# Fused attention and gated MLP on one core: one transfer out and four back for the reciprocals, new transfer durations in the planner, and a new order

## The chip, the cores and the metric

The kernel runs on one core of one Trainium2 chip. The metric is device time in microseconds, the median of several executions; lower is better. One execution was profiled, and its trace is read below.

## The reference, cut to what matters

There are 8 batches, 8 heads, 576 positions and a head size of 64; the MLP has d_model 512 and d_ff 1024. All arithmetic is in float32.

```python
q_rot, k_rot = (rotate(q), rotate(k))
scores = scale * np.matmul(q_rot, k_rot.transpose(0, 1, 3, 2))
scores = scores - np.max(scores, axis=-1, keepdims=True)
attn = np.exp(scores)
attn = attn / (np.sum(attn, axis=-1, keepdims=True) + 1e-09)
x = np.matmul(attn, v)            # then heads side by side: [8, 576, 512]
h = np.maximum(x @ w_in, 0.0)
u, v = (h[..., :d_ff // 2], h[..., d_ff // 2:])
v_n = (v - mu) / np.sqrt(var + 1e-06)
v_s = np.einsum('ts,bsd->btd', w_spatial, v_n) + b_spatial[None, :, None]
out = (u * v_s) @ w_out
```

## The kernel before

**The work.** The 64 heads are taken as 32 pairs, four pairs to a batch. A pair `i` loads its q and k (`st`, 576 KB each) and its values (`vr`), rotates them on GpSimd, splits them into a rounded high part and a rest, and copies the parts into the stacked operands `stk` by ten transfers inside SBUF. Its scores are nine tiles of 128 queries by 576 keys on TensorE (L782, for the first four pairs L802). VectorE takes the maximum of each row (L825), ScalarE the exponential and its row sum (L828), VectorE a transposition in blocks of 32 (L830), and TensorE multiplies with the values (L741). The first four pairs (`i < PLAIN`, which is 4) transpose on TensorE and multiply in L710. Four pairs make a batch's x, and `mlp(b)` then runs four groups of products on TensorE: L901, L924, L942 and L957.

**The normalisation.** The nine columns of row sums of a pair stand in `sums`, 128 partitions by 9. `normalise(i, ...)` (L832 on) adds 1e-9, takes the reciprocal (L862), transposes blocks of 32 by 32 into `rt` (L863), writes `rt` to a scratch in DRAM with `put`, reads it back with `get` as rows broadcast over 64 partitions into `rb`, and multiplies (L867). `put` issues six transfers of 128-byte or 64-byte pieces (eight for the first four pairs): one for each quarter of the partitions, and the ends of the rows apart. `get` issues two, one for each head, of 64 rows of 2304 bytes.

**The queue.** All transfers are issued by SyncE (SP) from one line, L416, in one order, and each occupies SP while it is issued. A transfer whose data are not there yet holds up all that stand behind it on SP.

**The order.** Every instruction is an `Op` with a duration, a key and the engines that may run it. `Program.run` plays the whole kernel through in a small model when the kernel is built: on each engine the ready instruction with the smallest key that finds its buffers goes next, and the order so found is the program's order on that engine. The durations are constants in the code: `dma_ns(kib, n, each, rate)` has `n` issues of `each` ns and `kib * rate` ns on the wire, `LATENCY[DMA]` follows, and `late` is added for some (`LATE` for q and k from the fifth pair on, `FIRST` for the first loads). The keys are the pair's number times 20 plus constants (`K_*`, `DEC_*`, `MOE_START` and others). So a constant of the model has no duration on the chip by itself; it sets who goes first.

Of the kernel before, what the change touches and what calls it, by code (L numbers as in the profile page):

```python
# [9 lines left out]
F32 = mybir.dt.float32  # L10
# [6 lines left out]
P = 128  # L17
S = 576
# [11 lines left out]
PE, ACT, DVE, POOL, DMA = "pe", "act", "dve", "pool", "dma"  # L30
LATENCY = {PE: 200, ACT: 142, DVE: 118, POOL: 95, DMA: 1880}
TO_PE = 104
LATE = 1244
AHEAD = 1564
BATCH, AHEAD_OF, IN_FLIGHT = 256, 32, 8
FIRST = 1100
FETCH_MIN, FETCH_END, FETCH_LANE, SLOW, STALL = 1456, 2550, 830, 1800, 187
SLOTS = {
    "stage": 3, "lk": 1, "vrep": 1, "et": 2, "x32": 1, "xg": 7, "m": 4,
    "stk": 3, "small": 3, "nmx": 3, "rt": 2, "sc": 2, "pm": 4, "eh": 6,  # L40
}
PSUM = {"sc": 1024, "pm": 512}
MOE_START, MOE_LENGTH = 90.78, 84.11
DEC_V = [16.2, 52.43, 33.76, 122.51]
DEC_S = [55.69, 17.44, 127.61]
DEC_U = [76.72, 127.06, 141.75, 112.54]
DEC_O = [120.69, 119.26, 149.95, 144.74]
GATE_U = [2, 2, 3, 3]
GATE_O = [3, 3, 4, 4]

# [5 lines left out]
PLAIN = 4  # L56
# [1 line left out]
    ([(0, 0), (1, 0), (0, 1), (1, 1), (0, 2), (1, 2)], [(0, P, 0, 0, 384)]),  # L58
    ([(0, 3), (1, 3), (0, 4)], [(0, 64, 0, 384, 192), (64, P, 0, 512, 64), (64, P, 64, 384, 128)]),
]  # L60
KT_STEP2 = [2.17, -10.78]
VALUES_AT2 = [16.33, -61.11]
K_HI, K_MUL, K_HALF = 24.71, 3.41, -61.86
WHOLE = 4
HOMES = [("stk", "stk"), ("stk", "stage"), ("stage", "stage"), ("xg", "xg")]
K_LOADW = 31.58
RESERVE = True
SCORE_SLOTS = [4, 3, 3, 3]
Q0 = 3 * TW
EARLY = 5  # L70
STEAL = 17.68
S_STEP = 2.14
K_MAX, K_EXP, K_TURN, K_AV, K_COPY = 0.75, 16.06, 0.83, 16.58, -29.43
K_LOAD, K_ROPE, K_SUM, K_HIQ, K_LOQ, K_LOK, K_STACK, K_STACK2 = -7.39, -83.67, 26.32, -12.65, -1.19, 73.16, 10.97, 57.55
K_TAIL = -46.85
K_INV, K_GET, K_X, K_XHI, K_XLO = 20.81, 41.14, 22.26, 71.21, 23.69
K_NORM, K_RELU, K_GATE, K_GHI, K_GLO, K_OB, K_OUT = 1.9, 11.65, -57.38, 64.16, -48.3, 2.06, 67.64


def pe_ns(n, m=P):  # L80
# [19 lines left out]
def dve_ns(n):  # L100
    return 68 + n * 25 // 24
# [49 lines left out]
class Program:  # L151
# [169 lines left out]
def tile_attention_gated_mlp(  # L321
# [18 lines left out]
    dr = ctx.enter_context(tc.tile_pool(name="dr", bufs=1, space=bass.MemoryType.DRAM))  # L340
# [5 lines left out]
    def make(b):  # L346
        tag = f"{b.pool}{b.slot}"
        if b.pool == "eh":
            return turns.tile[:, b.slot * CW:b.slot * CW + CW]
        if b.pool in PSUM:  # L350
            c0 = PSUM[b.pool] * b.slot
            return psum[:, c0:c0 + PSUM[b.pool] * b.wide]
        if b.pool == "rt":
            b.scratch = dr.tile([2, 5, P], F32, tag=tag, name=b.name + "d", bufs=1)
        return sb.tile(b.shape, b.dt, tag=tag, name=b.name, bufs=1)

    psum = ps.tile([P, 4096], F32, tag="psum", name="psum", bufs=1)
# [1 line left out]
    op = prog.op  # L359
# [55 lines left out]
    def load(dst, src):  # L415
        nc.sync.dma_start(out=dst, in_=src)  # L416
# [77 lines left out]
    def load_values(vr, b, hp, key):  # L494

        if vr.shape[1] == NQ * 2 * D:
            op(DMA, dma_ns(320, rate=2.2), key - K_LOAD + 1, lambda: load(vr.tile, v[b, hp].rearrange("p k h d -> p (k h d)")), w=[vr], new=[vr])
            return

        def fetch():  # L500
            rows = v[b, hp].rearrange("(q j) k h d -> j q (k h d)", q=4)
            for g in range(4):
                load(vr[32 * g:32 * g + 32].rearrange("j q k h d -> j q (k h d)"), rows)

        op(DMA, dma_ns(1280, 4, 470, 5.23), key - K_LOAD + 1, fetch, w=[vr], new=[vr])
# [11 lines left out]
    def prepare(i):  # L517
        b, hp = pairs[i]
        key = 20 * i
        if i < WHOLE:  # L520
            return prepare_whole(i, b, hp, key)
        st = [Buf("stage", [P, 2 * S], F32, f"st{i}_{j}") for j in range(2)]
        lk = Buf("lk", [P, 2 * S], F32R, f"lk{i}")
        vr = values_tile(i)
# [21 lines left out]
            pair_op(S, key - K_SUM, f, first=eng, r=[(st[j], 1)], w=[(st[j], 0)])  # L546

        for j in range(2):
            o = op(DMA, dma_ns(576, rate=3.26), key - K_LOAD, lambda j=j: load(st[j][:, :2 * S], qk[b, hp, j].rearrange("p c n -> p (c n)")), w=[(st[j], 0), (st[j], 1)], new=[st[j]])
            o.late = LATE if i >= 4 else 0  # L550
        load_values(vr, b, hp, key)
        for j, eng, part in ROPE0 if b == 0 else ROPE:
# [11 lines left out]
        for a in range(2):  # L564
            own = slice(64 * a, 64 * a + 64)
            oth = slice(64 - 64 * a, P - 64 * a)
            qd, kd, ld = lambda a=a: qs[a], lambda a=a: ks[a], lambda a=a: lks[a]
            for dst, rows, part, tok, dep in (
                (qd, own, 1, ("qs", a, 0), (st[0], 1)), (kd, own, 1, ("ks", a, 0), (lk, 1)), (kd, oth, 1, ("ks", a, 1), (lk, 1)),
                (ld, own, 0, ("lks", a), (lk, 0)), (qd, oth, 0, ("qs", a, 1), (st[0], 0)),  # L570
            ):
                def copy(dst=dst, rows=rows, own=own, part=part, src=dep[0], c0=a * TW if dst is qd else 0, n=4 * P if dst is qd else S):
                    load(dst()[rows, :].bitcast(F32), src[own, S * part + c0:S * part + c0 + n].bitcast(F32))

                op(DMA, dma_ns(132, 1, 570, 2.9), key - (K_STACK2 if a else K_STACK), copy, r=[dep], w=[tok])

    def prepare_whole(i, b, hp, key):

        q, k = (Buf(HOMES[i][j], [P, 2 * S], F32, f"st{i}_{j}") for j in range(2))
        vr = values_tile(i)  # L580
# [9 lines left out]
        if i == 0:  # L590
# [3 lines left out]
                return lambda: load(c2(dst)[:, :, cols], src[:, :, cols])  # L594

            def first(rank, kib, f, **kw):
                op(DMA, dma_ns(kib), rank - 70, f, **kw).late = FIRST
# [234 lines left out]
    def normalise(i, sm, x32, key):  # L832
        rt = Buf("rt", [P, 32], F32, f"rt{i}")
        rb = Buf("m", [P, S], F32, f"rb{i}")
        x = Buf("xg", [P, 2 * S + TW], F32R, f"x{i}")
        xs.append(x)
        need = [("sums", i % 2, c) for c in range(9)]

        def put():
            main = rt.scratch[:, :4, :]  # L840
            for j in range(4):
                load(main[:, :, 32 * j:32 * j + 32], rt[32 * j:32 * j + 8, :])
            ends = rt.scratch[:, 4, :64]
            if i < PLAIN:
                for h in range(2):
                    for j in range(2):
                        load(ends[h:h + 1, 32 * j:32 * j + 32], rt[64 * h + 32 * j + 8:64 * h + 32 * j + 9, :])
            else:
                for h in range(2):
                    load(ends[h].rearrange("(g k) -> g k", g=4), rt.tile.rearrange("(g r) n -> g r n", r=32)[:, 8, 16 * h:16 * h + 16])  # L850

        def get():
            for h in range(2):
                row = rt.scratch[h].rearrange("t p -> (t p)").rearrange("(o n) -> o n", o=1)
                load(rb[64 * h:64 * h + 64, :], row[:, :S].to_broadcast([64, S]))

        def low(e):
            rest_lo(e, x[:, S + TW:], x32.tile, x[:, :S])
            rest_lo(e, x[:, S:S + TW], x32[:, 4 * P:], x[:, 4 * P:S])

        op(ACT, 100, key + K_INV, lambda: nc.scalar.activation(sm[:, 0:9], sm[:, 0:9], AF.Copy, bias=1e-9), w=need)
        op(DVE, 205, key + K_INV, lambda: nc.vector.reciprocal(out=sm[:, 0:9], in_=sm[:, 0:9]), w=need)  # L862
        op(DVE, 125, key + K_INV, lambda: nc.vector.transpose(out=rt.tile, in_=sm), r=need, w=[rt], new=[rt])  # L863
        op(DMA, dma_ns(5, 8 if i < PLAIN else 6, 330, 120), key + K_INV, put, r=[rt], w=[(rt, 1)])
        op(DMA, dma_ns(288, 2, 590, 5.2), key + K_GET, get, r=[(rt, 1)], w=[rb, "rbs"], new=[rb])
        whole = [(x32, 0), (x32, 1)]
        pair_op(S, key + K_X, lambda e: e.tensor_tensor(out=x32.tile, in0=x32.tile, in1=rb.tile, op=ALU.mult), r=[rb], w=whole)  # L867
        op(ACT, 573, key + K_XHI, lambda: round_hi(x[:, :S], x32.tile), r=whole, w=[(x, 0)], new=[x])
        pair_op(S, key + K_XLO, low, pieces=2.8, r=[*whole, (x, 0)], w=[(x, 1)])


    def mlp(b):
# [38 lines left out]
        for t in range(NQ):  # L911
            pm, key = rows(t)
# [35 lines left out]
        for m in range(4):  # L948
            ob = Buf("m", [P, S], F32, f"ob{b}_{m}")
# [153 lines left out]
```

## Time and profile before

| | |
|---|---|
| median of 3 runs | 834.79 us (834.74 to 836.71) |
| profiled execution, its own time | 833.13 us |
| span of its trace | 831.4 us |
| TensorE busy | 801.3 us, 96% of the span |
| VectorE, ScalarE, GpSimd busy | 596.6, 525.3, 525.5 us |

The span runs from the first to the last instruction. A busy share is the time in which an engine had at least one instruction in work; an engine that waits inside a group of pipelined matmuls still counts as busy. The chain of waits follows the work that ended last back from the end, at each step to what released it. "SPq" is SP issuing a transfer, and "DMA a<-b" the time from there to its landing.

### The profile page before, as it was taken

What the parts mean: (1) busy time and instruction counts of PE and PEld (TensorE: products, weight loads), DVE (VectorE), ACT (ScalarE), POOL (GpSimd) and SP (SyncE); (2) the same over time, 40 slices, a digit from 0 to 9 for tenths busy, and PEclk for the clock granted to TensorE, in tenths of its full rate; (3) what the DMA queues carried; (4) which work ended last, traced back from release to release, by engine and by line L of the source; (5) the groups of instructions that cost most, each with busy time, mean ns of one, the idle gap of its engine ahead of it and who ended that gap; (6) DMA issues with size and microseconds to landing.
All of it is one profiled execution on the core that took longest, in us unless ns stands there. A gap on an engine that the chain in (4) does not pass through costs nothing.

```text
span 831.4 us, 30188 instructions
## 1 busy us (share of the span) xinstructions
PE 801.3 (96%) x12560; PEld 721.1 (87%) x12560; DVE 596.6 (72%) x1179; ACT 525.3 (63%) x1372; POOL 525.5 (63%) x440
## 2 busy tenths in 40 slices
PE   5999988999999999999999999999999999999998
PEld 3565678898899989998889989899899998999898
DVE  6879988886887669867686768776697766875220
ACT  4787877664865568656675648656586565844442
POOL 5998685786675667676566756767486675533221
PEclk9999999999999999999999999999999999999999
DMA  8755574779876777878847786777857778363001
GB/s 326 288 169 166 122 201 122 180 181 222 195 187 167 198 181 181 205 190 226 202 126 193 183 229 171 196 174 193 213 130 205 194 202 207 93 157 86 35 2 58
DMA packets 63867, 144.56 MB, mean 174 GB/s; under 512 B 10993, under 2 KB 12785, under 8 KB 63730
## 3 DMA queue, kind: packets, MB, share of 16 engines
q1 hardware_dynamic: 63730, 142.63, 66.3%
q8 instruction: 99, 1.62, 0.9%
q14 instruction: 38, 0.31, 0.1%
HBM read 93.55 MB, written 9.58 MB: 124 GB/s over the span
## 4 chain that ended last, share of the span: by engine, by line
PE 74%; DVE 7%; ACT 7%; DMA 5%; issue 3%; POOL 2%; SPq 1%; DVEq 0%; ACTq 0%; POOLq 0%
PE psum L741 15%; PE psum L942 14%; PE psum L782 13%; PE psum L957 10%; PE psum L901 9%; PE psum L924 7%; ACT et L828 4%; DMA vr<-in_v_dram 3%; DVE nmx L825 3%; PE psum L802 3%; PE psum L664 2%; PE psum L710 2%; DVE et L830 1%; SPq L416 1%; DVE sm L979 1%
## 5 line engine op out<-in xcount | busy, mean ns | idle before, releaser
L828 ACT ACTIVATE et<-psum,nmx 128x576 f32<-128x576 f32 x288 | 212.7, 740 | 111.1 <-DVE nmx L825 109.3
L825 DVE TENSOR_REDUCE nmx<-psum 128x1 f32<-128x576 f32 x288 | 210.9, 744 | 74.4 <-PE psum L782 64.7
L830 DVE STREAM_TRANSPOSE et<-et 128x576 f32<-128x576 f32 x252 | 192.7, 770 | 42.8 <-ACT et L828 40.7
L541 POOL TENSOR_TENSOR st<-st,tabs 128x576 f32<-128x576 f32 x112 | 163.0, 1468 | 64.1 <-DMA st<-in_qk_dram 49.5
L741 PE MATMUL psum<-et,vr 32*64 32x144 f32 x8064 | 142.7, 285 | 4.1 <-ACT vv L975 1.4
L741 PEld LDWEIGHTS psum<-et,vr 32*64 32x64 f32 x8064 | 126.8, 130 | 17.0 <-issue 11.1
L942 PE MATMUL psum<-wsp,vn 128*128 128x288 f32 x768 | 125.0, 296 | 1.2 <-issue 1.2
L924 PE MATMUL psum<-x,wi 128*128 128x288 f32 x768 | 118.9, 296 | 0.0
L957 PE MATMUL psum<-g,wo 128*128 128x288 f32 x768 | 117.4, 296 | 0.2
L901 PE MATMUL psum<-wi,x 128*128 128x512 f32 x448 | 117.6, 397 | 0.0
L942 PEld LDWEIGHTS psum<-wsp,vn 128*128 128x128 f32 x768 | 109.4, 188 | 2.6 <-issue 2.6
L924 PEld LDWEIGHTS psum<-x,wi 128*128 128x128 f32 x768 | 108.0, 188 | 3.8 <-issue 1.6
L957 PEld LDWEIGHTS psum<-g,wo 128*128 128x128 f32 x768 | 106.5, 188 | 2.5 <-issue 2.4
L782 PE MATMUL psum<-stk 128*128 128x288 f32 x448 | 99.4, 303 | 8.7 <-ACT et L828 8.3
L782 PE MATMUL psum<-stk,stk 128*128 128x288 f32 x448 | 95.7, 295 | 0.1
L901 PEld LDWEIGHTS psum<-wi,x 128*128 128x128 f32 x448 | 79.6, 188 | 16.4 <-issue 2.6
L422 POOL TENSOR_TENSOR g<-u,g 128x288 fp32r<-128x288 f32 x64 | 52.0, 816 | 63.7 <-ACT g L419 63.6
L782 PEld LDWEIGHTS psum<-stk 128*128 128x128 f32 x448 | 72.8, 188 | 19.8 <-ACT et L828 13.2
L545 POOL TENSOR_TENSOR st<-st 128x576 f32<-128x576 f32 x56 | 82.6, 1476 | 2.0
L422 POOL TENSOR_TENSOR vn<-vv,vn 128x512 fp32r<-128x512 f32 x32 | 41.3, 1293 | 61.8 <-ACT vn L419 61.8
L782 PEld LDWEIGHTS psum<-stk,stk 128*128 128x128 f32 x448 | 71.6, 188 | 0.2 <-issue 0.2
L422 POOL TENSOR_TENSOR x<-x,x 128x576 fp32r<-128x576 f32 x64 | 55.6, 890 | 17.2 <-ACT x L419 17.1
(134 smaller groups left out, 1012.3 us busy)
## 6 DMA issues: line engine op xcount, KB each, us to landing
vr<-in_v_dram SPq DMA_DIRECT2D x116, 320.0 KB
st<-in_qk_dram SPq DMA_DIRECT2D x62, 576.0 KB
stk<-lk SPq DMA_DIRECT2D x168, 144.0 KB
stk<-st SPq DMA_DIRECT2D x112, 128.0 KB
out_dram<-ob SPq DMA_DIRECT2D x31, 288.0 KB
ws<-in_w_spT_dram SPq DMA_DIRECT2D x2, 576.0 KB
st<-in_qk_dram SPq DMA_DIRECT2D x2, 288.0 KB
tabs<-in_tab_dram SPq DMA_DIRECT2D x2, 288.0 KB
```

The source lines that it names most:

```text
L422: eng.tensor_tensor(out=lo, in0=src, in1=hi.bitcast(F32), op=ALU.subtract)
L541: f = lambda e: e.tensor_tensor(out=st[j][:, cols], in0=st[j][:, cols], in1=tabs[:, cols], op=ALU.mult)
L545: f = lambda e: e.tensor_tensor(out=st[j][:, :S], in0=st[j][:, :S], in1=st[j][:, S:2 * S], op=ALU.add)
L741: nc.tensor.matmul(bank(g)[64 * h:64 * h + 64, EACH // 9 * (1 - h):EACH // 9 * (1 - h) + EACH], lhsT=vr[rows, b % 4, b // 4, h, :], rhs=e[ ...
L782: nc.tensor.matmul(pt[:, c * 512:c * 512 + HALF], lhsT=lhsT, rhs=rhs[:, c * HALF:(c + 1) * HALF], start=(n == 0), stop=(n == len(parts) - 1))
L825: op(DVE, 680, key + K_MAX, lambda: nc.vector.tensor_reduce(out=nmx.tile, in_=tops(), op=ALU.max, axis=AX.XY, negate=True), r=[pt], w=[nmx ...
L828: op(ACT, 750, key + K_EXP, lambda: nc.scalar.activation(weights(), tops(turn), AF.Exp, bias=nmx.tile, scale=1.0, accum_out=sm[:, to:to + ...
L830: op(DVE, 705, key + K_TURN, lambda: nc.vector.transpose(out=blocks(et, at), in_=blocks(et, at)), w=[(et, at)])
L901: nc.tensor.matmul(pm.tile, lhsT=lhsT, rhs=win[1, d][:, j, :], start=(d == 0 and n == 0), stop=(d == 3 and n == len(todo) - 1))
L924: nc.tensor.matmul(pm[:, :HALF], lhsT=win[0, d][:, i, f * P:(f + 1) * P], rhs=x[d][:, at:at + HALF], start=(d == 0 and n == 0), stop=(d == ...
L942: nc.tensor.matmul(pm[:, :HALF], lhsT=lhsT, rhs=rhs, start=(t == 0 and n == 0), stop=(t == 4 and n == 1))
L957: nc.tensor.matmul(pm[:, :HALF], lhsT=wout[d,][:, i, m * P:(m + 1) * P], rhs=gs[d][:, at:at + HALF], start=(d == 0 and n == 0), stop=(d == ...
```

## The change

`put` becomes one transfer: all 32 rows of `rt` go out, 128 pieces of 128 bytes, into a scratch whose row r holds column block r of all 128 partitions. `get` becomes four: for each head a row of 512 reciprocals broadcast over 64 partitions (64 pieces of 2048 bytes), and the last 64 apart, as 64 pieces of 256 bytes for the first four pairs and as 256 pieces of 64 bytes for the other 28. The planner's durations of transfers are changed, with two of the first loads' latency, and the constants of the order are other ones. No instruction of TensorE, VectorE, ScalarE or GpSimd is added or removed.

```diff
-LATE = 1244
+LATE = 500
...
-FIRST = 1100
+FIRST = 1300
...
-MOE_START, MOE_LENGTH = 90.78, 84.11
-DEC_V = [16.2, 52.43, 33.76, 122.51]
+MOE_START, MOE_LENGTH = 92.7314, 83.2345
+DEC_V = [23.2885, 13.3177, 44.4713, 120.3521]
...
-K_LOADW = 31.58
+K_LOADW = 13.9176
...
-STEAL = 17.68
-S_STEP = 2.14
-K_MAX, K_EXP, K_TURN, K_AV, K_COPY = 0.75, 16.06, 0.83, 16.58, -29.43
+STEAL = 26.7661
+S_STEP = 1.5294
+K_MAX, K_EXP, K_TURN, K_AV, K_COPY = 3.5716, 7.799, 4.251, -9.9358, -125.7552
...
-K_INV, K_GET, K_X, K_XHI, K_XLO = 20.81, 41.14, 22.26, 71.21, 23.69
+K_INV, K_GET, K_X, K_XHI, K_XLO = 23.0945, -0.7648, 152.9607, 183.8042, 33.8908
...
-            b.scratch = dr.tile([2, 5, P], F32, tag=tag, name=b.name + "d", bufs=1)
+            b.scratch = dr.tile([32, P], F32, tag=tag, name=b.name + "d", bufs=1)
...
-        op(DMA, dma_ns(1280, 4, 470, 5.23), key - K_LOAD + 1, fetch, w=[vr], new=[vr])
+        op(DMA, dma_ns(1280, 4, 470, 4.6), key - K_LOAD + 1, fetch, w=[vr], new=[vr])
...
-                op(DMA, dma_ns(132, 1, 570, 2.9), key - (K_STACK2 if a else K_STACK), copy, r=[dep], w=[tok])
+                op(DMA, dma_ns(132, 1, 630, 4.4), key - (K_STACK2 if a else K_STACK), copy, r=[dep], w=[tok])
...
         def put():
-            main = rt.scratch[:, :4, :]
-            for j in range(4):
-                load(main[:, :, 32 * j:32 * j + 32], rt[32 * j:32 * j + 8, :])
-            ends = rt.scratch[:, 4, :64]
-            if i < PLAIN:
-                for h in range(2):
-                    for j in range(2):
-                        load(ends[h:h + 1, 32 * j:32 * j + 32], rt[64 * h + 32 * j + 8:64 * h + 32 * j + 9, :])
-            else:
-                for h in range(2):
-                    load(ends[h].rearrange("(g k) -> g k", g=4), rt.tile.rearrange("(g r) n -> g r n", r=32)[:, 8, 16 * h:16 * h + 16])
+            load(rt.scratch.rearrange("r (g n) -> g r n", g=4), rt.tile)
 
         def get():
             for h in range(2):
-                row = rt.scratch[h].rearrange("t p -> (t p)").rearrange("(o n) -> o n", o=1)
-                load(rb[64 * h:64 * h + 64, :], row[:, :S].to_broadcast([64, S]))
+                row = rt.scratch[4 * h:4 * h + 4, :].rearrange("t p -> (t p)").rearrange("(o n) -> o n", o=1)
+                load(rb[64 * h:64 * h + 64, :4 * P], row.to_broadcast([64, 4 * P]))
+                ends = rt.scratch[8:9, :]
+                ends = ends[:, 64 * h:64 * h + 64].to_broadcast([64, 64]) if i < PLAIN else ends.rearrange("o (g h n) -> o h g n", g=4, h=2)[:, h].to_broadcast([64, 4, 16])
+                load(rb[64 * h:64 * h + 64, 4 * P:], ends)
...
-        op(DMA, dma_ns(5, 8 if i < PLAIN else 6, 330, 120), key + K_INV, put, r=[rt], w=[(rt, 1)])
-        op(DMA, dma_ns(288, 2, 590, 5.2), key + K_GET, get, r=[(rt, 1)], w=[rb, "rbs"], new=[rb])
+        op(DMA, dma_ns(5, 1, 650, 80), key + K_INV, put, r=[rt], w=[(rt, 1)])
+        op(DMA, dma_ns(288, 4, 585, 5.4), key + K_GET, get, r=[(rt, 1)], w=[rb, "rbs"], new=[rb])
```

Left out above are further constants of the order, and four durations of the same kind: loads of q and k go from 3.26 to 4.0 ns per KiB, stores of the output from 2.0 to 2.9, the first loads get 630 ns an issue, and the first rotation on VectorE 210 ns more.

## Rows read from the trace of the kernel before

**Rows 1.** The page: span, busy time of each engine, DMA packets, SP's queue.

```profile
span 831.4 us, 30188 instructions
...
PE 801.3 (96%) x12560; PEld 721.1 (87%) x12560; DVE 596.6 (72%) x1179; ACT 525.3 (63%) x1372; POOL 525.5 (63%) x440
...
DMA packets 63867, 144.56 MB, mean 174 GB/s; under 512 B 10993, under 2 KB 12785, under 8 KB 63730
...
q1 hardware_dynamic: 63730, 142.63, 66.3%
```

**Rows 2.** Five stretches: length, each engine's busy time, granted clock, DMA share, GB/s.

```profile
0.00:20.80 20.80, 10.91 (x49) 6.39 (x49) 13.06 (x19) 9.10 (x20) 12.48 (x22) 1.00 0.89 327
20.80:83.10 62.30, 60.02 (x445) 36.28 (x446) 53.30 (x92) 49.35 (x124) 55.33 (x43) 0.97 0.63 208
83.10:166.30 83.20, 75.62 (x1264) 65.44 (x1263) 71.29 (x145) 60.45 (x155) 57.77 (x48) 1.00 0.64 156
166.30:769.00 602.70, 595.60 (x10405) 556.69 (x10404) 445.44 (x878) 382.96 (x1019) 385.18 (x315) 1.00 0.73 182
769.00:831.40 62.40, 59.19 (x404) 56.34 (x402) 13.53 (x49) 23.42 (x58) 14.70 (x15) 0.99 0.08 31
```

**Rows 3.** Whom TensorE waited for, whole span: total us, times, longest.

```profile
PE psum L782 <- ACT et L828: 8.6, 11, 1.6
PE psum L802 <- DVE st L614: 7.8, 1, 7.8
```

**Rows 4.** SP's timeline, 60 to 130 us: start, length, transfers issued together.

```profile
83.64 3.90 SPq L416 DMA_DIRECT2D rt3d<-rt  x8
87.96 1.15 SPq L416 DMA_DIRECT2D rb<-rt3d  x2
...
103.43 0.58 SPq L416 DMA_DIRECT2D st<-in_qk_dram  x1
104.44 3.68 SPq L416 DMA_DIRECT2D rt4d<-rt  x6
108.23 0.39 SPq L416 DMA_DIRECT2D st<-in_qk_dram  x1
```

**Rows 5.** SP's timeline, 500 to 530 us.

```profile
521.31 3.71 SPq L416 DMA_DIRECT2D rt21d<-rt  x6
...
529.08 1.14 SPq L416 DMA_DIRECT2D rb<-rt21d  x2
```

**Rows 6.** Line L416: issue times on SP, shortest/median/longest in ns.

```profile
L416 SPq DMA_DIRECT2D stk<-lk x168: 461/596/1493, 71.8 to 737.2; - x168
L416 SPq DMA_DIRECT2D vr<-in_v_dram x116: 317/432/1507, 6.9 to 747.2; - x116
...
L416 SPq DMA_DIRECT2D rt5d<-rt x6: 504/567/673, 135.9 to 139.1; - x6
```

**Rows 7.** The chain of waits, 80 to 130 us: shares, and two pieces.

```profile
by line: DMA vr<-in_v_dram 13.9%; DMA st<-in_qk_dram 11.5%; POOL st L541 11.2%; SPq L416 8.5%; issue 7.1%; DVE vv L978 6.3%; DMA rb<-rt3d 5.0%; POOL vn L422 4.8%; DVE nmx L825 4.2%; PE psum L782 3.7%; ACT et L828 3.3%; POOL st L545 2.9%; PO
...
86.72 1.05 DMA rt3d<-rt
...
87.96 2.48 DMA rb<-rt3d
```

**Rows 8.** The chain of waits, whole span: three transfers in it after 166 us.

```profile
420.18 2.16 DMA stk<-st
...
530.89 4.80 DMA vr<-in_v_dram
...
598.52 5.25 DMA vr<-in_v_dram
```

**Rows 9.** The stretches of 20.8 us around those three transfers, columns as in rows 2.

```profile
415.70:436.50 20.80, 19.53 (x397) 18.70 (x396) 17.85 (x37) 15.89 (x44) 13.17 (x11) 1.00 0.46 126
...
519.60:540.40 20.80, 19.89 (x396) 18.66 (x395) 16.61 (x31) 13.53 (x37) 15.85 (x12) 1.00 0.75 195
...
582.00:602.80 20.80, 19.44 (x369) 16.75 (x368) 12.79 (x27) 10.53 (x29) 9.48 (x8) 1.00 0.83 213
```

More of the change, by code (lines that the diff above doesn't have):

```diff
@@ L42 @@
 PSUM = {"sc": 1024, "pm": 512}
-MOE_START, MOE_LENGTH = 90.78, 84.11
-DEC_V = [16.2, 52.43, 33.76, 122.51]
-DEC_S = [55.69, 17.44, 127.61]
-DEC_U = [76.72, 127.06, 141.75, 112.54]
-DEC_O = [120.69, 119.26, 149.95, 144.74]
+MOE_START, MOE_LENGTH = 92.7314, 83.2345
+DEC_V = [23.2885, 13.3177, 44.4713, 120.3521]
+DEC_S = [103.407, 26.1658, 115.2645]
+DEC_U = [83.0234, 115.1148, 137.4423, 92.8763]
+DEC_O = [121.7361, 108.2366, 254.3817, 225.7783]
 GATE_U = [2, 2, 3, 3]
@@ L60 @@
 ]
-KT_STEP2 = [2.17, -10.78]
-VALUES_AT2 = [16.33, -61.11]
-K_HI, K_MUL, K_HALF = 24.71, 3.41, -61.86
+KT_STEP2 = [2.2251, -132.2217]
+VALUES_AT2 = [15.9616, -143.3999]
+K_HI, K_MUL, K_HALF = 25.5559, 4.4162, -82.7595
 WHOLE = 4
 HOMES = [("stk", "stk"), ("stk", "stage"), ("stage", "stage"), ("xg", "xg")]
-K_LOADW = 31.58
+K_LOADW = 13.9176
 RESERVE = True
@@ L70 @@
 EARLY = 5
-STEAL = 17.68
-S_STEP = 2.14
-K_MAX, K_EXP, K_TURN, K_AV, K_COPY = 0.75, 16.06, 0.83, 16.58, -29.43
-K_LOAD, K_ROPE, K_SUM, K_HIQ, K_LOQ, K_LOK, K_STACK, K_STACK2 = -7.39, -83.67, 26.32, -12.65, -1.19, 73.16, 10.97, 57.55
-K_TAIL = -46.85
-K_INV, K_GET, K_X, K_XHI, K_XLO = 20.81, 41.14, 22.26, 71.21, 23.69
-K_NORM, K_RELU, K_GATE, K_GHI, K_GLO, K_OB, K_OUT = 1.9, 11.65, -57.38, 64.16, -48.3, 2.06, 67.64
+STEAL = 26.7661
+S_STEP = 1.5294
+K_MAX, K_EXP, K_TURN, K_AV, K_COPY = 3.5716, 7.799, 4.251, -9.9358, -125.7552
+K_LOAD, K_ROPE, K_SUM, K_HIQ, K_LOQ, K_LOK, K_STACK, K_STACK2 = -29.0819, -103.2473, 15.1342, -111.9707, -5.3568, 51.5141, 75.935, 74.9394
+K_TAIL = -126.5927
+K_INV, K_GET, K_X, K_XHI, K_XLO = 23.0945, -0.7648, 152.9607, 183.8042, 33.8908
+K_NORM, K_RELU, K_GATE, K_GHI, K_GLO, K_OB, K_OUT = 5.181, 1.3722, -93.1305, 44.8406, -85.003, -23.8649, 84.9935
 def pe_ns(n, m=P):
@@ L548, in prepare @@
         for j in range(2):
-            o = op(DMA, dma_ns(576, rate=3.26), key - K_LOAD, lambda j=j: load(st[j][:, :2 * S], qk[b, hp, j].rearrange("p c n -> p (c n)")), w=[(st[j], 0), (st[j], 1)], new=[st[j]])
+            o = op(DMA, dma_ns(576, rate=4.0), key - K_LOAD, lambda j=j: load(st[j][:, :2 * S], qk[b, hp, j].rearrange("p c n -> p (c n)")), w=[(st[j], 0), (st[j], 1)], new=[st[j]])
             o.late = LATE if i >= 4 else 0
@@ L596, in first @@
             def first(rank, kib, f, **kw):
-                op(DMA, dma_ns(kib), rank - 70, f, **kw).late = FIRST
+                op(DMA, dma_ns(kib, 1, 630), rank - 70, f, **kw).late = FIRST
             first(0, 288, lambda: part(k.tile, qk[b, hp, 1], halves[0])(), w=[(k, 0)], new=[k])
@@ L621, in prepare_whole @@
                 n = cols.stop - cols.start
-                op(DVE, dve_ns(2 * n) + dve_ns(n), rank - 60, lambda f=f, cols=cols: f(cols), r=need, w=[t], port=True)
+                op(DVE, dve_ns(2 * n) + dve_ns(n) + 210, rank - 60, lambda f=f, cols=cols: f(cols), r=need, w=[t], port=True)
         else:
@@ L964, in mlp @@
                 continue
-            op(DMA, dma_ns(288, rate=2.0), key + K_OUT, lambda m=m, ob=ob: load(out[b, m * P:(m + 1) * P, :], ob.tile), r=[(ob, 0), (ob, 1)])
+            op(DMA, dma_ns(288, rate=2.9), key + K_OUT, lambda m=m, ob=ob: load(out[b, m * P:(m + 1) * P, :], ob.tile), r=[(ob, 0), (ob, 1)])
     def norm(b, t, pm, key, sum_halves):
```

## The prediction

> **What bounds the kernel now.** I read the page first, for who is busy. TensorE is busy 801.3 of 831.4 us, and no other engine is above 72% [rows 1]. So the kernel ends when TensorE's list is through, and a change that adds and removes no instruction of TensorE can only move the time in which TensorE stands. That time is span less busy time, and the view of stretches tells where it lies [rows 2]. From 0 to 20.8 us it is 20.80 - 10.91 = 9.89 us, from 20.8 to 83.1 us 2.28, from 83.1 to 166.3 us 7.58, from 166.3 to 769 us 7.10, and in the end 3.21; together 30.06. The table of waits names the largest single one: 7.8 us before the first matmul, which waits for the rotated q of the first pair [rows 3]. It also says that the commonest wait is for the exponential (8.6 us in 11 times, 1.6 at most), so that ScalarE and VectorE feed TensorE just in time. The granted clock was 1.00 in three of the five stretches and 0.97 and 0.99 in the others [rows 2], so no term stands for the clock.
>
> The reader is to see two things in this. First, a ceiling: without the first and the last stretch, which hold the start and the drain, 2.28 + 7.58 + 7.10 = 17.0 us are left, 2% of the time. Second, a place: the stretch from 83.1 to 166.3 us, where the kernel goes over from the first four pairs to the stacked ones and the first MLP begins, loses 9% of its length, and the 600 us behind it 1.2%.
>
> Next I read the chain of waits in the worst stretch. From 80 to 130 us it runs through transfers and their issue more than through TensorE: values 13.9%, loads of q and k 11.5%, SP issuing 8.5%, reading the reciprocals back 5.0%, together 38.9% [rows 7]. Then I read SP's own timeline, because the reciprocals' transfers stand in its queue ahead of the loads: eight of them take 3.90 us from 83.64, and six take 3.68 us from 104.44, between two loads of q and k at 103.43 and 108.23 [rows 4].
>
> **The change, part by part.** *One transfer out.* Six issues take 3.71 us of SP [rows 5], 567 ns the median one [rows 6]; eight take 3.90 [rows 4]. The one that replaces them is of 128 pieces. No row has this shape; the loads of the values, also of 128 pieces in a form of three dimensions, take 432 ns to issue and the copies into the stack 596 [rows 6]. Between 0.43 and 0.67 us, the longest of the old puts [rows 6], I take 0.65. SP gains 3.1 us a pair for 28 pairs and 3.3 for the other four.
>
> *Four transfers back.* Two take 1.14 us [rows 5], so one takes 0.57; four take 2.3 and SP loses 1.2 us a pair. The net gain is 1.9 us of SP a pair, some 60 us over 32 pairs.
>
> *Landing.* The last of the eight puts landed 1.05 us after its issue ended [rows 7], and the first had been issued at 83.64: the reciprocals could be read at 87.96, 4.3 us later [rows 4]. With one put it is 0.65 us of issue and a landing of 1.05 us or more. How much more is not shown: the old ones had few pieces on a transfer, the new one 128. Bounds are 1.05 us and the 4.80 us in which one of the loads of 128 pieces landed that are twenty times longer [rows 8]. It is nearer to the old puts in size, and I take 2 us; then the read is released 1.6 us earlier (4.3 - 2.7), and 1.2 us of that goes into its two additional issues. The multiplication behind it gains about 0.4 us, next to nothing. What stays is SP's time: loads behind the put in the queue start up to 3.1 us earlier, those behind the get 1.9.
>
> *Small pieces.* From the fifth pair on the ends come back as 512 pieces of 64 bytes a pair. What a piece costs the DMA engines is not shown, so it is bounded. By bytes: 32 KB of 142.63 MB, which took 66.3% of 831.4 us on each of 16 engines [rows 1], is 0.13 us a pair. By count: 551 us times 16 over 63730 packets is 138 ns a packet, and 512 of those on 16 engines are 4.4 us a pair. The old puts are the row that is nearest, pieces of 64 and 128 bytes, and the last of eight landed 1.05 us behind its issue [rows 7]; that includes the whole way there, so I stay near the low end with 0.5 us. That is less than the 1.9 us SP gains, and the engines were 73% busy in the long stretch [rows 2], so it finds room.
>
> The Trainium skill speaks against this part: DMA: Bandwidth & Descriptors, section Specifications, gives 512 bytes as the least piece at line rate and says that smaller ones go through a read-modify-write. By this rule the pieces would lie toward the dear end, and the time would be that of the rival of small pieces below; the rows here show no count of such pieces on the way back, so they neither agree nor disagree.
>
> *The plan's durations and the keys.* These have no time on the chip by themselves. Six puts were planned at 6 times 330 ns and took 3.71 us [rows 5]; the new plan has 650 ns for one and 585 for each get, near the rows. A copy into the stack was planned at 570 ns of issue and took 596 [rows 6], and 630 holds the gap behind it too. So the new plan's queue is closer to SP's, and its choices of order will be less often upset by a queue that runs late. But the order itself is a new one of some 60 changed constants, and no row shows it. Its bounds are the 17.0 us that are there to gain, and on the other side as many new waits as a plan can have: I price them below.
>
> *The sum.* Start: no term, since the first loads are not behind a put; bounds 0 and half a microsecond either way. Stretch 20.8 to 83.1: its 2.28 us are VectorE's and TensorE's doing (four pairs whose loads are early), no term. Stretch 83.1 to 166.3: of 7.58 us, 38.9% went through transfers and their issue, and both puts of this stretch stand in front of loads; 0.39 times 7.58 is 3.0 us saved, bounds 0 and 7.6. The long stretch: three places where the chain goes through a transfer (a copy at 420.18, values at 530.89 and 598.52 [rows 8]) lie in slices that stand 1.27, 0.91 and 1.36 us [rows 9], 3.54 together; SP's gain of 1.9 us would reach each, but a load also waits for its buffer, so I take half, 1.8; bounds 0 and 7.1. Sum 4.8 us. The profiled execution took 833.13 us, 1.7 beside its span; 833.1 - 4.8 = 828.3. The median of the runs is 1.7 us above that execution, so 830.0, 0.6% below 834.8.
>
> **The rivals.** A measurement of this kernel can tell about 0.3% from no change, that is 2.5 us: 832.3 to 837.3.
>
> *Hidden.* TensorE's waits are mostly for the exponential [rows 3], and SP's queue is no part of those. Then the transfers' gain stays off the path and the new order comes out as good as the old: 833 to 836, 834.5. For it speaks that the long stretch is 98.8% busy; against it the 38.9% of rows 7.
>
> *A better order.* A plan with truer durations also removes waits for the exponential in the bad stretch. Two thirds of the 17.0 us gone is 11 us: 823.5. Against it: the old order had already brought 600 us to 1.2%.
>
> *A worse order.* The new keys let the scores' softmax run late more often. Each time TensorE stands up to 1.6 us [rows 3]. If one such wait more comes in each of the 8 batches, that is 12.8 us, less the 4.8 saved: 842.8; with four or five, 837.5 to 840. It decides for slower from five such waits on. For it speaks that the order is all new; against it the truer queue.
>
> *Small pieces.* The 512 pieces cost 4.4 us a pair, and net of SP's 1.9 that delays the values and copies by 2.5 us at the places where the chain goes through them: the bad stretch and three behind it, 10 us together, 844.8. It passes the gain from 1.9 us a pair, which is 1.9 times 16 over 512, 59 ns a piece.
>
> **How the numbers follow.** The forecast (826.5 to 832.3, likeliest 830.0) gets 0.42, since both its terms have rows but the order may drown them. Better order: 0.14 (818 to 826.5). Hidden: 0.22. Worse order: 0.14 (837.3 to 843). Small pieces: 0.08 (839 to 847). So faster 0.56, same 0.22, slower 0.22. Leaving out the lower third of the better order and most of the upper halves of the two slower cases, together some 0.15, gives 822.5 to 841.0.
>
> **What would show it.** SP's timeline should have one put of 0.5 to 0.7 us and four gets of 2.2 to 2.5 us a pair, and fewer than 700 transfers. A put should land within 3 us; its read should be released at most 3 us behind the reciprocals' transposition. The stretch where the stacked pairs begin should stand 4 to 5 us in place of 7.58, and the long one 5 to 6 in place of 7.10, with TensorE's busy time within 2 us of 801.3. Reading back should not land later than it did, and the DMA share of the long stretch should stay within 0.03 of 0.73; a share near 0.85 would mean the small pieces. The prediction is wrong if TensorE's standing time grows outside the bad stretch, which would be the order, or if busy time itself moves by more than 3 us, because then the order of matmuls costs something that this account of waits leaves out.

## The result and the profile after

The kernel after takes 845.64 us (843.97 to 849.28, 4 runs), the one before 835.75 in the same series: a ratio of 1.0122, 95% interval 1.0084 to 1.0161. It is slower by 1.2%, where 0.6% faster was forecast, and lies 4.6 us above the range. The profiled execution took 845.92 us, with a span of 844.1. That of the kernel before took 833.13 us, 2.6 below that median, so the two spans lie further apart (12.7 us) than the two medians (9.9).

The page of the kernel after, for [rows 1]; q8 is the queue that brings instructions:

```profile
span 844.1 us, 30142 instructions
...
PE 809.1 (96%) x12560; PEld 727.5 (86%) x12560; DVE 585.4 (69%) x1178; ACT 526.6 (62%) x1373; POOL 526.1 (62%) x440
...
DMA packets 82202, 144.94 MB, mean 172 GB/s; under 512 B 29329, under 2 KB 31121, under 8 KB 82066
...
q1 hardware_dynamic: 82066, 143.01, 66.6%
q8 instruction: 99, 1.62, 0.8%
...
L741 PE MATMUL psum<-et,vr 32*64 32x144 f32 x8064 | 150.3, 288 | 10.5 <-issue 7.0
```

The same group on the page of the kernel before:

```profile
L741 PE MATMUL psum<-et,vr 32*64 32x144 f32 x8064 | 142.7, 285 | 4.1 <-ACT vv L975 1.4
```

Of the 12.7 us that the span grew, TensorE stands 844.1 - 809.1 = 35.0 us in place of 30.1, so 4.9 of them, and is busy 7.8 us longer with the same 12560 matmuls. The group L741 alone has 7.6 us more of busy time and 6.4 more of idle time ahead of it, 14.0 together; the rest of TensorE gave 1.3 back. L741 runs in two halves of 144 matmuls a pair, and two halves hold over 8 of these 14 us, from the first matmul's start to the last one's end: the first half of pair 4 takes 9.07 us for 4.42 before, and the second of pair 6 takes 6.16 for 2.51. So the reader is to look at L741, and at why a fixed number of matmuls is busy for longer.

Stretches of the kernel after, for [rows 2]:

```profile
83.10:166.30 83.20, 77.24 (x1069) 66.48 (x1072) 71.02 (x146) 60.18 (x158) 59.77 (x48) 0.94 0.64 159
166.30:769.00 602.70, 591.95 (x10307) 552.84 (x10290) 436.23 (x876) 383.52 (x1016) 383.99 (x314) 1.00 0.75 183
```

Its slices around the change to stacked pairs, and a later one:

```profile
84.40:105.50 21.10, 16.89 (x126) 11.49 (x125) 20.46 (x36) 17.70 (x48) 16.06 (x13) 0.95 0.47 113
105.50:126.60 21.10, 19.65 (x340) 16.56 (x341) 14.82 (x33) 8.95 (x22) 8.97 (x7) 0.81 0.75 181
168.80:189.90 21.10, 18.16 (x246) 17.42 (x246) 14.49 (x25) 10.27 (x25) 15.85 (x15) 0.92 0.64 152
```

The last three columns are the granted clock, the DMA share and GB/s. Before, the stretch from 83.1 us had a clock of 1.00 [rows 2]. Now TensorE stands over 4 us in the slice from 84.4, and the mean clock is 0.81 in the next: part of that slice ran at 1.2 GHz in place of 2.4. From 104 to 113 us the granted clock is 0.50, and again from 175 to 178 us, in the third of these slices. In the long stretch TensorE stands 602.70 - 591.95 = 10.75 us in place of 7.10.

Whom TensorE waited for in the kernel after, for [rows 3]:

```profile
PE psum L802 <- DVE st L614: 8.6, 2, 7.8
PE psum L741 <- issue: 7.0, 10, 2.3
PE psum L741 <- DMA vr<-in_v_dram: 3.4, 4, 1.1
PE psum L782 <- ACT et L828: 3.2, 4, 1.9
PE psum L664 <- ACT et L828: 3.1, 3, 2.5
```

The waits of L782 for the exponential fell from 8.6 to 3.2 us: the new order does what a planner can see, though L664's for the same rose from 0.3 to 3.1. Two others came: L741 for "issue", that is for nothing that the profile shows, and L741 for the values of a pair. In the kernel before the first of these was small:

```profile
PE psum L741 <- issue: 0.8, 2, 0.5
```

TensorE's timeline of the kernel after, from 98 us, shows the second one, and what the clock did to it:

```profile
101.06 0.53 PE L782 MATMUL psum<-lk,qt 128*128 128x288 f32 x2 [1.93 <-ACT et L828]
...
103.22 0.66 PE L741 MATMUL psum<-et,vr 32*64 32x144 f32 x2 [1.10 <-DMA vr<-in_v_dram]
104.64 0.73 PE L741 MATMUL psum<-et,vr 32*64 32x144 f32 x2 [0.75 <-DMA vr<-in_v_dram]
106.21 0.73 PE L741 MATMUL psum<-et,vr 32*64 32x144 f32 x2 [0.83 <-DMA vr<-in_v_dram]
107.68 4.61 PE L741 MATMUL psum<-et,vr 32*64 32x144 f32 x138 [0.74 <-DMA vr<-in_v_dram]
...
114.22 2.51 PE L741 MATMUL psum<-et,vr 32*64 32x144 f32 x144
```

The first multiplication of a stacked pair waits for each of its four loads of values, and then its 138 matmuls take 4.61 us where the next 144 take 2.51. The clock had gone down by then: it is 0.64 from 103 to 104 us and 0.50 behind that. Before it fell TensorE had stood 1.93 us for the exponential and 1.10 for the first load; the other three waits for values, 2.32 us, came at the lower clock. In the kernel before TensorE had work of the first MLP for that time:

```profile
97.84 5.73 PE L901 MATMUL psum<-wi,x 128*128 128x512 f32 x24
```

And from 164 us, a wait without a releaser in the middle of a group, twice:

```profile
165.11 2.51 PE L741 MATMUL psum<-et,vr 32*64 32x144 f32 x144
...
168.67 0.48 PE L741 MATMUL psum<-et,vr 32*64 32x144 f32 x10
169.81 2.27 PE L741 MATMUL psum<-et,vr 32*64 32x144 f32 x128 [0.66 <-issue]
174.36 0.47 PE L741 MATMUL psum<-et,vr 32*64 32x144 f32 x6 [2.29 <-issue]
```

Right behind the second of them the clock is at 0.50 once more, so such a wait, too, came before a fall of the clock.

SP's timeline of the kernel after, for [rows 4, 5]:

```profile
85.87 0.57 SPq L416 DMA_DIRECT2D rt3d<-rt  x1
87.90 2.40 SPq L416 DMA_DIRECT2D rb<-rt3d  x4
...
98.49 2.35 SPq L416 DMA_DIRECT2D vr<-in_v_dram  x4
```

### The profile page after: what moved, and what is told of

Its sections match the earlier page's. It is cut to its first block, busy times and chain, and to the rows that moved or that the text cites. A ratio compares the mean times of both kernels' runs of the same rounds, so it can differ in the third digit from the quotient of the medians.

```text
span 844.1 us, 30142 instructions
## 1 busy us (share of the span) xinstructions
PE 809.1 (96%) x12560; PEld 727.5 (86%) x12560; DVE 585.4 (69%) x1178; ACT 526.6 (62%) x1373; POOL 526.1 (62%) x440
## 5 line engine op out<-in xcount | busy, mean ns | idle before, releaser
L541 POOL TENSOR_TENSOR st<-st,tabs 128x576 f32<-128x576 f32 x112 | 163.4, 1470 | 40.0 <-DMA st<-in_qk_dram 16.4
L741 PE MATMUL psum<-et,vr 32*64 32x144 f32 x8064 | 150.3, 288 | 10.5 <-issue 7.0
L741 PEld LDWEIGHTS psum<-et,vr 32*64 32x64 f32 x8064 | 130.3, 132 | 26.7 <-issue 18.5
L935 PE MATMUL psum<-wsp,vn 128*128 128x288 f32 x768 | 122.2, 297 | 0.0
L782 PE MATMUL psum<-stk 128*128 128x288 f32 x448 | 99.4, 303 | 2.5 <-ACT et L828 1.3
L782 PE MATMUL psum<-stk,stk 128*128 128x288 f32 x448 | 96.4, 297 | 0.0
L782 PEld LDWEIGHTS psum<-stk 128*128 128x128 f32 x448 | 74.2, 189 | 12.3 <-issue 3.4
L860 POOL TENSOR_TENSOR x<-x,rb 128x576 f32<-128x576 f32 x32 | 46.3, 1445 | 43.2 <-DVE x L759 32.3
L782 PEld LDWEIGHTS psum<-stk,stk 128*128 128x128 f32 x448 | 72.5, 190 | 0.0
```

Source lines behind the costliest of these rows:

```text
L541: f = lambda e: e.tensor_tensor(out=st[j][:, cols], in0=st[j][:, cols], in1=tabs[:, cols], op=ALU.mult)
L741: nc.tensor.matmul(bank(g)[64 * h:64 * h + 64, EACH // 9 * (1 - h):EACH // 9 * (1 - h) + EACH], lhsT=vr[rows, b % 4, b // 4, h, :], rhs=e[ ...
L782: nc.tensor.matmul(pt[:, c * 512:c * 512 + HALF], lhsT=lhsT, rhs=rhs[:, c * HALF:(c + 1) * HALF], start=(n == 0), stop=(n == len(parts) - 1))
L935: nc.tensor.matmul(pm[:, :HALF], lhsT=lhsT, rhs=rhs, start=(t == 0 and n == 0), stop=(t == 4 and n == 1))
```

## The experiments

The first theory was that the order carries the loss. Its rivals were the new transfers (their small pieces or landings), and the planner's new durations. Each run has a kernel before on its own chip; the ratio is to that.

| run | median us | ratio | interval |
|---|---|---|---|
| e1 new order, old transfers | 854.99 | 1.0215 | 1.0166 to 1.0264 |
| e2 old order, new transfers | 841.26 | 1.0074 | 1.0051 to 1.0096 |
| e3 old keys, new durations and transfers | 867.71 | 1.0387 | 1.0347 to 1.0426 |
| e4 new keys, old durations and transfers | 857.69 | 1.0271 | 1.0227 to 1.0315 |
| e5 old order, ends in whole rows | 842.94 | 1.0070 | 1.0033 to 1.0107 |
| e6 old order, no transfers of reciprocals | 836.94 | 1.0017 | 0.9991 to 1.0044 |
| e7 new order, ends in whole rows | 844.89 | 1.0092 | 1.0057 to 1.0126 |
| e8 old order, one constant nudged | 840.03 | 1.0036 | 1.0013 to 1.0058 |
| e9 before, TensorE's list shifted by 128 | 862.51 | 1.0328 | 1.0287 to 1.0368 |
| e10 before, shifted by 256 | 838.13 | 1.0038 | 1.0019 to 1.0058 |
| e11 after, values of pair 4 early | 841.34 | 1.0081 | 1.0053 to 1.0108 |
| e12 after, shifted by 128 | 867.40 | 1.0403 | 1.0360 to 1.0446 |
| e13 e11 shifted by 24 | 846.58 | 1.0119 | 1.0067 to 1.0171 |
| e14 e11 shifted by 48 | 853.40 | 1.0190 | 1.0138 to 1.0242 |
| e15 e11 shifted by 208 | 854.98 | 1.0222 | 1.0160 to 1.0284 |
| e16 e11 shifted by 232 | 848.35 | 1.0142 | 1.0088 to 1.0196 |
| e17 e11, halves of L741 apart | 843.14 | 1.0086 | 1.0069 to 1.0104 |
| e18 before, halves of L741 closer | 837.27 | 1.0023 | 0.9990 to 1.0056 |

### Order or transfers

`e1` gives the kernel after its old `put` and `get` back; `e2` gives the kernel before the new ones. The planner's counts stay, so that every engine's order is that of the kernel it came from, but for SP's puts and gets.

```diff
# e2, in the kernel before; e1 is the reverse in the kernel after
-                load(main[:, :, 32 * j:32 * j + 32], rt[32 * j:32 * j + 8, :])
...
+            load(rt.scratch.rearrange("r (g n) -> g r n", g=4), rt.tile)
```

> The order of the kernel after on every engine, with the six or eight transfers out and two back of the kernel before; the planner still counts the new ones, so only SP's puts and gets differ from the kernel after. Order theory (the loss is in the order: first stacked multiplication waiting for its values, the clock that fell behind it, TensorE out of instructions in L741): 844 to 848 us, the put's SP time of 1.9 us a pair on top at most here and there. Transfer theory (small pieces or landings of the new transfers hold up loads or the instruction fetch): back to 834 to 838.

> The order of the kernel before on every engine, with the one transfer out and four back; only SP's puts and gets differ from the kernel before. Order theory: 832 to 836, a gain of 0 to 3 us from SP's 1.9 us a pair. Transfer theory: 842 to 848, with L741 standing for instructions as in the kernel after.

Neither theory alone fits; each median lies outside both of its ranges. The new order with the old transfers is 2.15% above before, worse than the kernel after: under this order the new transfers are a gain of 0.9%, some 8 us. Under the old order they are a loss of 0.7%, 6 us. TensorE's waits in e2, with the same list of matmuls as before, show what moved:

```profile
PE psum L741 <- issue: 5.8, 6, 1.7
```

L741's wait without a releaser was 0.8 us in the kernel before. So changing the transfers alone brings L741 such waits, under an unchanged order. That these are the 6 us is not shown: the profiled execution of e2 took 836.22 us, the least of its ten and inside the range of the kernel before, so where its median of 841.26 loses time stands in no trace.

The gain that SP made did arrive, but at GpSimd. Its wait for q and k (L541), in the kernel before, in e2 and in the kernel after:

```profile
L541 POOL TENSOR_TENSOR st<-st,tabs 128x576 f32<-128x576 f32 x112 | 163.0, 1468 | 64.1 <-DMA st<-in_qk_dram 49.5
...
L541 POOL TENSOR_TENSOR st<-st,tabs 128x576 f32<-128x576 f32 x112 | 163.2, 1470 | 22.4 <-DMA st<-in_qk_dram 13.2
...
L541 POOL TENSOR_TENSOR st<-st,tabs 128x576 f32<-128x576 f32 x112 | 163.4, 1470 | 40.0 <-DMA st<-in_qk_dram 16.4
```

With the order unchanged the loads come early enough to take 36 us off GpSimd's waits, and TensorE gains nothing by it.

### Keys or durations

`e3` puts the old constants of the order into the kernel after; `e4` puts the new ones into the kernel before.

```diff
# e3, in the kernel after, and so on for all keys
-K_MAX, K_EXP, K_TURN, K_AV, K_COPY = 3.5716, 7.799, 4.251, -9.9358, -125.7552
+K_MAX, K_EXP, K_TURN, K_AV, K_COPY = 0.75, 16.06, 0.83, 16.58, -29.43
```

> The new transfers and the planner's new durations, with the keys of before. If the keys carry the loss: 832 to 839. If the new durations steer the planner wrong: 842 or more.

> The old transfers and the planner's old durations, with the new keys. If the keys carry the loss: 842 or more. If the new durations carry it: 832 to 839. If a pair of keys and durations works only together, this one and the run with old keys and new durations are both above 840.

Both are well above 840, and above the kernel after, as was expected if keys and durations work as a pair; that any change of so many constants costs as much is not excluded. L741 waits 10.3 us for "issue" in e3 and 11.8 in e4. This says of neither that it carries the loss; it says that one can't be judged without the other.

### Small pieces, and no transfers at all

`e5` and `e7` read the last 64 reciprocals of each row as one row of 256 bytes for all pairs, in the old and the new order.

```diff
-                ends = ends[:, 64 * h:64 * h + 64].to_broadcast([64, 64]) if i < PLAIN else ends.rearrange("o (g h n) -> o h g n", g=4, h=2)[:, h].to_broadcast([64, 4, 16])
+                ends = ends[:, 64 * h:64 * h + 64].to_broadcast([64, 64])
```

`e6` is the kernel before without `put` and `get`, with `in1=x32.tile` in L867.

> The order of before with the new transfers, as the second run, but the ends come back for all pairs as 64 pieces of 256 bytes a transfer in place of 256 pieces of 64 bytes (the last 64 queries of later pairs get other positions' reciprocals). If the small pieces cost: back to 834 to 836 from 841. If what costs is that the instruction supply of TensorE falls elsewhere in L741: 838 to 844 again.

> The kernel after with 64 pieces of 256 bytes for the ends of all pairs (same remark on the last 64 queries). If the small pieces cost: 836 to 841. If not: 842 to 850.

> The order of before without any transfer of reciprocals; the multiplication of L867 takes x32 twice (x is not normalised). If the transfers are a load that costs: 835 at most, likely 830 to 833. If the order only fits the timing of the transfers that it was set with: 836 to 843 although 264 transfers are gone, with over 3 us of L741 waiting for instructions.

Pieces of 64 bytes cost nothing over pieces of 256 that can be measured: e5 (1.0070) is where e2 is (1.0074), and e7 (1.0092) and the kernel after (1.0122) lie within each other's intervals. The old transfers are no load either: without any of them the old order takes 0.17% more, with an interval that holds zero, and L741 waits for "issue" again:

```profile
PE psum L741 <- issue: 6.5, 9, 1.1
```

Of the transfer theory the small pieces fall with this, and the rest does not: under the old order the new transfers are slower than none (e2 1.0074 to e6 1.0017, with intervals apart), and what in them costs that is open. That 264 transfers less gain nothing agrees with an order that is set to the landings it had; that the one pays for the other is argued, not shown. And e6 says that L741's waits are not the loss by themselves: it has 6.5 us of them, near the 7.0 of the kernel after, at a time that can't be told from before.

### Is the old order a lucky one

`e8` changes `S_STEP` from 2.14 to 2.15 in the kernel before.

> The kernel before with one constant of the order nudged, S_STEP from 2.14 to 2.15; old transfers, old durations. If the old order is one of many that are about as good: 833 to 838. If it is a lucky one among its neighbours: 840 to 855, with more of L741 waiting for instructions.

It costs 0.36%, and its median lies at the lower edge of the range given for a lucky order. The one neighbour that was timed is a little worse, not 2% worse; luck among neighbours explains a part at most, as far as one neighbour tells. Its L741 waits 1.8 us for "issue", so that part of the expectation missed.

### Is it the instruction supply

TensorE's list has about 25,000 instructions in the trace, a weight load and a matmul in turn, and q8 brought 99 packets of 16 KB: one for some 255 instructions. L741 has matmuls of 32 rows and takes 288 instructions in 2.5 us; other lines take that long for about 20 matmuls. The times in the trace of the kernel after join the two: all ten waits of L741 for "issue" end 1.22 to 1.50 us behind the end of a packet on q8, while these packets end 8.2 us apart in the mean. The one of 2.29 us ends at 174.36 us, and a packet had ended at 172.89; the one of 0.66 ends at 169.81, and a packet at 168.31. If L741's waits without a releaser are waits for the next packet, then a shift of the whole list must move them. `e9`, `e10` and `e12` put tiny matmuls ahead of the first real one, where TensorE waits 7.8 us for its data anyway.

```diff
     with tc.manual_schedule():
+        shift = T([32, 32], F32, "shift")
+        nc.vector.memset(shift, 0.0)
+        for n in range(64):
+            nc.tensor.matmul(psum[0:32, 3584:3586], lhsT=shift.bitcast(F32R)[:, :32], rhs=shift.bitcast(F32R)[:, :2], start=True, stop=True)
         prog.run(make)
```

> The kernel before with 64 tiny matmuls of a zeroed tile on TensorE ahead of the first real one, in the 7.8 us in which it waits for its data; order, transfers and durations as before. If where TensorE's instruction fetches fall in its list matters: 837 to 844, with over 3 us of L741 waiting for instructions in place of 0.8. If not: 834 to 836.

> The same with 128 tiny matmuls, which is 256 instructions, near the mean distance of two fetches in the trace of before (25291 instructions of TensorE in 99 fetches). If the place of the fetches matters: back to 834 to 837, better than with 64. If the tiny matmuls themselves cost: worse than with 64.

> The kernel after with the 64 tiny matmuls. If the new order's waits in L741 come from where the fetches happen to fall: a change of 2 us or more either way, with other L741 groups waiting than those at 171.8 and 293.8 us. If they belong to the order itself: 844 to 847 with the same ones.

Half a packet costs the kernel before 3.3%, and a whole one brings it back to 0.4%, although twice as many matmuls stand in front. The kernel after goes from 1.2% to 4.0%. TensorE's waits in e9 and e10:

```profile
PE psum L741 <- issue: 13.8, 12, 3.6
PE psum L942 <- issue: 4.7, 2, 2.7
...
PE psum L957 <- issue: 2.6, 1, 2.6
```

```profile
PE psum L741 <- issue: 1.3, 1, 1.3
```

So "issue" in the rows of L741 is TensorE out of instructions, and both orders are set to where the packets end. The planner does know of this (`Feed`, with `BATCH` 256), which fits that a shift it is not told of costs so much. The expectation for e9 was far too low, and e10 came out 1 us above its range; for e12 only "2 us or more" had been named, and it was some 22. The effect is larger than the whole loss under study.

### The values of the first stacked pair

In `e11` the four loads of pair 4's values go into memory of their own (that of `vn`, which is not in use yet) right behind its q and k; `vr4x` below is that memory. All else of the kernel after keeps its order.

```diff
+        if vr.name == "vr4":
+            early.append(lambda: fetch(spare()))
...
+            vals = spare() if i == 4 else vr
```

> The kernel after, but the values of the first stacked pair (pair 4) go into memory of their own and are loaded right behind its q and k; all else keeps its order. If the wait of the first L741 for its values and the clock that falls behind it carry a good part of the loss: 837 to 842, no wait for vr and a granted clock of 1.00 from 103 to 113 us. If they are only a symptom: 844 to 847.

TensorE's timeline of e11:

```profile
102.46 0.47 PE L759 MATMUL psum<-et,vr4x 32*64 32x144 f32 x8 [0.27 <-ACT et L846]
103.87 4.02 PE L759 MATMUL psum<-et,vr4x 32*64 32x144 f32 x136 [0.93 <-DVE et L848]
...
109.24 1.99 PE L759 MATMUL psum<-et,vr4x 32*64 32x144 f32 x108
112.86 0.95 PE L759 MATMUL psum<-et,vr4x 32*64 32x144 f32 x36 [1.63 <-issue]
```

The wait for values is gone, and the median falls by 4.3 us to 841.34, by the ratios 3.4 us; since the two intervals overlap, the size is known only roughly. The clock did not hold at 1.00 as expected (0.96 in the stretch from 83.1 to 166.3, 0.94 in the kernel after), and 136 matmuls still take 4.02 us. TensorE had stood 1.93 us for the exponential at 101 us, as in the kernel after, and 0.93 for the transposition just ahead; that this is what the clock fell for is argued. What remains is L741 (L759 here):

```profile
PE psum L759 <- issue: 8.1, 11, 2.0
```

### Could a small shift mend the rest

`e13` to `e16` add 12, 24, 104 and 116 of the tiny matmuls to e11.

> The kernel after with the values of pair 4 early, and 12 tiny matmuls (24 instructions) ahead. If the rest of the loss is the place of the fetches: a change of over 2 us against 841.3 in some of these four, both signs, with the time following L741's wait for instructions. If it is the order: 840 to 843 in all four.

> The same with 24 tiny matmuls (48 instructions later). Place: as above, farther out and so rather worse, 843 to 850. Order: 840 to 843.

> The same with 104 tiny matmuls (208 instructions, near 48 earlier). Place: 838 to 850. Order: 840 to 843.

> The same with 116 tiny matmuls (232 instructions, near 24 earlier). Place: 836 to 845. Order: 840 to 843. If one of the four is below 834, it beats both kernels.

None is better, and they go in order of distance: from 1.0081 unshifted to 1.0119 and 1.0142 at 24 instructions to either side, whose intervals still overlap with that of e11, and 1.0190 and 1.0222 at 48, which are clear of it. L741's waits go along, 8.1, 8.1 and 8.6, then 13.1 and 14.5 us. So of the five places timed the new order already stands at the best; that a wrong place is what it suffers from found no support. e13's expectation, a change of both signs, missed, and the other three lie above both of their ranges.

### Are the halves of L741 too close

L741 runs in two halves of 288 instructions. `e17` lets the second half of pairs 6, 15 and 22 in e11 go behind the next group on TensorE; `e18` in the kernel before lets the first half of five pairs go behind three matmuls of L901.

```diff
# in Program.run
-                    chosen.f(e)
+                    if e == PE and chosen.hold:
+                        parked.append([chosen.hold, chosen.f])
+                    else:
+                        chosen.f(e)
...
# e17, in attention; e18 has the hold on the first half, for pairs 12, 16, 20, 24, 28
+        op(PE, 2600, key + K_AV, lambda: multiply(half, NB), r=need, w=pv, count=32 * half).hold = 1 if i in (6, 15, 22) else 0
```

> The kernel after with the values of pair 4 early, and the second half of L741 of pairs 6, 15 and 22 moved behind the next group on TensorE, one scores tile or so (0.5 us); all else keeps its order. If halves too close outrun the instruction fetch: those three second halves fall from 6.0, 3.4 and 3.1 us to under 2.7, and the time by 2 to 5 us, to 836 to 839. If the distance is a coincidence: 840 to 844.

> The kernel before with three matmuls of L901 (0.7 us) moved from between the two halves of L741 to ahead of the first, in pairs 12, 16, 20, 24 and 28, whose halves start 4.0 to 4.1 us apart; all else as before. If halves too close outrun the fetch: second halves of 2.8 us or more in at least three of the five, and 837 to 842. If not: 834 to 836.

Pair 15 in TensorE's timeline of e11:

```profile
383.59 2.51 PE L759 MATMUL psum<-et,vr 32*64 32x144 f32 x144
...
387.54 1.43 PE L759 MATMUL psum<-et,vr 32*64 32x144 f32 x66
389.71 1.50 PE L759 MATMUL psum<-et,vr 32*64 32x144 f32 x78 [0.73 <-issue]
```

The same pair in e17, where the line is L769:

```profile
385.43 2.51 PE L769 MATMUL psum<-et,vr 32*64 32x144 f32 x144
...
390.37 0.52 PE L810 MATMUL psum<-stk 128*128 128x288 f32 x2 [0.93 <-ACT et L856]
...
391.08 2.51 PE L769 MATMUL psum<-et,vr 32*64 32x144 f32 x144
```

Apart, the second half runs without a gap, here and in pair 22 (3.43 us in e11, 2.51 now), but not in pair 6, where it still takes 5.56 us (6.25 in e11). And the scores that now go first wait for the exponential. Over the span of e17:

```profile
PE psum L810 <- ACT et L856: 7.9, 6, 3.0
PE psum L769 <- issue: 4.3, 5, 1.4
```

L741's wait fell from 8.1 to 4.3 us and the scores' wait rose from 2.5 in e11 to 7.9; the time did not fall (1.0086). In e18 the second halves of the five pairs take 2.70, 3.16, 2.64, 3.02 and 2.97 us, where four of them took 2.51 before and the first 2.57, so closer halves do run into the supply, as was expected. The waits of L741 rose to 2.4 us, and the ratio of 1.0023 can't be told from 1. Distance is one of the things that let L741 outrun its supply, a small one, and mending it in e17 brought other waits in its place.

## Why the prediction was wrong

**What bounds the kernel.** TensorE's list sets the time: that stayed right. That a change without new matmuls can only move the time in which TensorE stands was wrong. Busy time grew by 7.8 us, through the clock (138 matmuls in 4.61 us) and through short stalls inside groups, which the view of stretches counts as busy: at 211.44 us 144 matmuls take 2.96 us in place of 2.51, at a clock of 1.00.

**The transfers.** The prices of issue were right: one put of 0.57 us for 0.65, four gets of 2.40 for 2.3. From the put's start to its read it is 87.90 - 85.87 = 2.0 us, where 2.7 was taken. The landing of the old puts had been read from the wrong one: the eight issues end at 87.54 [rows 4], and the 1.05 us from 86.72 [rows 7] is not the last one's; the sum did not use it. DMA share of the long stretch rose from 0.73 to 0.75, within the bound given. Pieces of 64 bytes cost nothing over pieces of 256 (e5, e7). The rule of the Trainium skill that was weighed there (DMA: Bandwidth & Descriptors, section Specifications: under 512 bytes a transfer loses line rate) is tested by no run here, since both sizes lie under it; that they come out alike (1.0074 and 1.0070) speaks only against a price that grows with the number of pieces.

**From SP's time to TensorE's.** This step failed. The sum credited SP's gain to TensorE at 3.0 us in the bad stretch and 1.8 in the long one. The 3.0 took the share of transfers in a chain of waits, 38.9%, for their share of the time in which TensorE stands; in the whole table that [rows 3] is cut from TensorE waits for no transfer at all. The gain went to GpSimd, whose wait for q and k fell from 49.5 to 16.4 us, and to 13.2 under the old order (e2), and stopped there. At the first put of the bad stretch not even the queue had it: it starts at 85.87 in place of 83.64, so its read stands at 87.90 where it stood at 87.96, and the gain is spent. In that stretch TensorE stands 83.20 - 77.24 = 5.96 us for 7.58, but at a clock of 0.94, so less work is done in it. In the long stretch it stands 10.75 us for 7.10.

**The order.** The step that decided was the term left at zero: that a plan with durations nearer to the trace would be "less often upset". The runs show the opposite of a small term. The same transfers save 8 us in one order and cost 6 in the other (e1, e2); e3 and e4 cost 3.9% and 2.7%. The rival of small pieces had the nearest time, 844.8, and the only range that holds 845.64, with a chance of 0.08; that is luck, since e5 and e7 show no such cost. The rival of a worse order, 842.8 with a chance of 0.14, had the right place and another mechanism: it counted waits for the exponential, and L782's fell to 3.2 us while L664's rose to 3.1. (By its own terms four or five such waits give 834.8 - 4.8 + 6.4 or 8.0, so 836.4 to 838.0, and not 837.5 to 840.) What rose were L741's waits for instructions, 0.8 to 7.0 us, and the first stacked pair's wait for values, 3.4 us, with the clock at half from the first of these on.

**What stays open.** In e11 the early values give back 3 to 4 us of the 10 (1.0122 to 1.0081, with intervals that overlap). For the rest, L741 is shown to wait for instructions, and neither a shift of the list, at the four distances timed, nor a wider gap in three pairs mended it. How much of the loss these waits are is open: e6 has 6.5 us of them and loses nothing that can be measured. Which keys make the new order so, and whether an order exists that has the shorter waits of L782 and the old ones of L741, was not settled. No run beat the kernel before.

## What to carry to other kernels

An order found by a planner holds for one set of transfers: time them together, and judge neither a transfer nor a duration by the other's order. Where the engine that sets the end runs many small instructions, read its waits for "issue" apart from all others, and count instructions, not only microseconds, in what a change moves ahead of them. A gain on a queue is worth what the next wait behind it leaves; price it at that wait, not at the queue. Here the next wait was GpSimd's, and GpSimd had time to spare.

## What was not expected of the hardware

- 128 more instructions ahead of TensorE's list, in time that was idle, cost 3.3% and 256 cost 0.4% (e9, e10); for the kernel after 128 took the ratio from 1.0122 to 1.0403.
- All ten waits of L741 for "issue" in the kernel after, 7.0 us, end 1.22 to 1.50 us behind the end of a packet of instructions.
- A wait cost more than itself: TensorE stood 1.93 and 1.10 us close behind each other, the granted clock was 0.50 from 104 to 113 us, and 138 matmuls took 4.61 us in place of 2.5. After 2.29 us without instructions it was 0.50 again, from 175 to 178 us.
- 14336 pieces of 64 bytes, 512 a pair for 28 pairs, on engines that were 75% busy: no cost over a quarter as many pieces of 256 bytes could be measured.
